# A banded attention and two feed-forward layers on one core: the order of a chunk's side jobs, with all float64 pieces ahead of both weights

## The chip, the cores and the metric

The kernel runs on 1 core of one Trainium2 chip. The metric is the device time of one execution in microseconds (us), as the median of several runs. The core's engines are named as in the profile: PE is the matrix engine (PEld its weight loads), DVE the vector engine, ACT the scalar engine, POOL the GpSimd engine, and SP the engine whose queue issues every DMA of this kernel.

## The reference, cut to what matters

Three layers follow each other on 2304 tokens of 512 values: an attention in which a query sees itself and the 127 positions before it, a layer of 8 experts whose gate is made doubly stochastic by 8 rounds of row and column scaling, and a dense layer with a leaky ReLU.

```python
for e in range(E):                       # E = 8 experts, F = 1024
    h = np.maximum(x @ w1[e], 0.0)
    out += P[:, e:e + 1] * (h @ w2[e])
...
h = x @ w_in                             # 512 x 2048
return np.maximum(0.01 * h, h) @ w_out   # 2048 x 512
```

The weights of the experts arrive as float32. The weights of the dense layer, `w_in` and `w_out`, arrive as float64, so the kernel turns them into float32 itself.

## The kernel before, in words

**The long stage.** After the attention, the kernel works through 20 chunks `ci`: 16 of them are halves of an expert (512 columns of `w1`, 512 rows of `w2`), the last 4 are quarters of the dense layer. The tokens are cut into five groups `p`; four hold two pairs of 128-token tiles and one, `p == 4`, holds one pair. For each chunk and group there is a first product (`a_steps`, L686 on) and a second one (`b_steps`, L817 on). Each product of 2 by 2 blocks is made with seven block products, each of them a "step" of six matmuls of 256 columns (twelve of 128 in the first product of group 4). A step's result is read out of PSUM by ACT and DVE, and the low halves of the float16 operands are made on POOL (L794).

**The order of units.** The main loop (L1015 to L1067) walks over units `(ci, p)`, from chunk 1 on in the order of `p` 0, 4, 1, 2, 3. A unit's first products are merged with the second products of the unit before it, so that the units 4, 1, 2, 3, 0 that follow each other have 21, 21, 28, 28 and 28 steps: 126 steps a chunk.

**Side jobs.** What is not on the way of the products is cut into small jobs in a list `side`. The list for the next chunk, `ci + 1`, is filled when unit `(ci, 4)` begins (L1041) and `tick` (L1055) hands out so many of them after each step that they are used up a fixed number of steps later:

```python
rest = {4: 57, 1: 36, 2: 8, 3: -19}.get(p) ...
tick(-(-len(side) // max(len(seq) - k + rest, 1)))
```

At the start of unit `(ci, 4)` that is 21 + 57 = 78 steps for the whole list. Where there are more jobs than steps, two jobs follow each of the first steps until the numbers are even. `pop` ties a job's instructions behind the last read-out that the steps have issued on each of ACT, DVE and POOL, so a job does not run earlier than its step; it can run later, since the program's final order on each engine is drawn up at compile time from when its inputs are expected. SP's loads and stores are not tied to steps: they stand in SP's queue in program order, and each waits there for its buffer.

**What the jobs do.** There are two kinds. A float64 piece (`to_single`, L628 to L680) is loaded as integers (512 KB, L644), goes through five jobs, `exponent` (DVE L650, ACT L653), `signed` (DVE L656), `high` (DVE L661, ACT L662), `low` (ACT L668, POOL L670) and `put` (POOL L674 and a store, L675), and ends in DRAM as float32. There are 32 pieces: three for each of the chunks 2 to 11, whose lists run during chunks 1 to 10, and two in the list that runs during chunk 11. The other kind are the chunk's two weights `a` (first product) and `b` (second product): a load of 1 MB (L565), then `scale()`, 16 or 17 jobs (four sums of squares on ACT, L569; a small reduction across partitions by way of PE and DVE, L421 to L441; four scalings on ACT, L572), then `early()`, 6 jobs (two splits into float16 halves, ACT L446 and POOL L447, and four block sums on POOL, L596). The remaining five splits of each weight (`at`) are made later, in the last steps of the chunk, as the weight tiles come free.

**The buffers.** Pieces and weights share two staging buffers, the tag `raw` of the pool `stg`. A piece gives its buffer back when its store has landed. A weight holds its buffer until its last split, at the end of the chunk. So of the five loads of a chunk's list, the first two wait for the two weights of the list before, and each other one waits for the store of a piece.

Of the kernel before, what the change touches and what calls it, by code (L numbers as in the profile page):

```python
# [31 lines left out]
def attn_moe_kernel(  # L32
# [591 lines left out]
    def weights(ci):  # L624
        for which in range(2):
            W[which][ci] = Weights(ci, which)
# [363 lines left out]
    def side_jobs(ci, n):  # L990

        todo = [to_single(cast.pop(0)) for _ in range(min(n, len(cast)))]
        weights(ci)
        a, b = W[0][ci], W[1][ci]
        jobs = [load for load, _ in todo[:2]]
        if not todo:
            return [a.load, b.load] + [None] * 10 + a.scale() + a.early() + b.scale() + b.early()
        jobs += [None] * 8 + todo[0][1] + [a.load]
        if len(todo) > 1:
            jobs += todo[1][1]  # L1000
        if len(todo) > 2:
            jobs += [todo[2][0]] + [None] * 4 + a.scale() + todo[2][1] + [b.load] + a.early()
        else:
            jobs += [b.load] + [None] * 8 + a.scale() + a.early()
        return jobs + [None] * 8 + b.scale() + b.early()

    def weigh(ci):
        pu[ci] = small.tile([P, NTILE], F32, tag="pu", name="pu")
# [12 lines left out]
    for n, u in enumerate(units + [None]):  # L1021
        a, b = [], b_steps(*prev)
        if u is not None:
            ci, p = u
            assert ci < NCE or p in split_pairs
            a = a_steps(ci, p)
            k0 = len(a) - 7
            if p == ends[ci] and ci + 1 < NC:
                a = [[f] + ([lambda j=k - k0: W[0][ci + 1].at(j)] if k >= k0 else []) for k, f in enumerate(a)]
            else:  # L1030
                a = [[f] for f in a]
        if prev[1] == ends[prev[0]] and prev[0] + 1 < NC:
            k0 = len(b) - 7
            b = [[f] + ([lambda j=k - k0: W[1][prev[0] + 1].at(j)] if k >= k0 else []) for k, f in enumerate(b)]
        else:
            b = [[f] for f in b]
        if u is not None and ci >= 1:
            if n and units[n - 1][0] != ci and ci != NCE:
                weigh(ci)
            if p == 4:  # L1040
                side += side_jobs(ci + 1, 3 if ci < NCE - 1 else 0) if ci + 1 < NC else []  # L1041
# [65 lines left out]
```

## Time and profile before

| | |
|---|---|
| median of 3 runs | 1924.01 us (1923.15 to 1927.62) |
| the profiled execution: its time | 1925.29 us |
| the profiled execution: its span | 1923.5 us |
| instructions in the span | 45099 |
| PE busy | 1852.1 us (96%) |
| ACT, DVE, POOL busy | 1363.4, 1314.2, 1325.4 us |
| granted PE clock over the span | 0.995 of full speed |

The span is the time from the first to the last instruction of the profiled execution; its own time is 1.8 us longer. A row of the timeline gives the start of an instruction, its duration, its engine, the line of the kernel, what it writes and reads, and in square brackets how long the engine had been idle before it and what ended the idle time. Matmuls are pipelined and their ends are modelled, so a short pause of PE shows less idle time than it costs; the period from one chunk to the next shows the whole.

### The profile page before, as it was taken

How to read it: one execution, taken by the hardware profiler on the slowest of the kernel's cores; microseconds unless marked ns; L12 is line 12 of the kernel's file. 1: busy time of each engine (PE TensorE's matmuls, PEld its weight loads, DVE VectorE, ACT ScalarE, POOL GpSimd, SP SyncE). 2: the span in 40 equal slices, each digit the busy share in tenths (PEclk: the TensorE clock that was granted, in tenths of full speed). 3: DMA queues.
4: the chain of work that ended last, by engine and by line, in shares of the span. 5: the costliest groups of instructions: out<-in, count | busy, mean ns of one | idle time of the engine just before them, and what ended most of it. 6: DMA issues, size and time to landing. Idle time of an engine off the chain costs nothing.

```text
span 1923.5 us, 45099 instructions
## 1 busy us (share of the span) xinstructions
PE 1852.1 (96%) x17725; PEld 1609.8 (84%) x17725; DVE 1314.2 (68%) x3606; ACT 1363.4 (71%) x3125; POOL 1325.4 (69%) x1142
## 2 busy tenths in 40 slices
PE   7899898999999999999999999999999998999998
PEld 5677787888888888988888888988889787888897
DVE  5456566766776767767676777666666786677776
ACT  7978667776767767676776767666666779776764
POOL 3843566867768686877868777685767786665753
PEclk8999999999999999999999999999999999999999
DMA  7522002021111202111111201100001010101001
GB/s 230 171 89 83 2 12 83 26 69 55 45 63 39 70 26 83 30 65 67 40 56 40 83 23 56 45 24 23 23 24 45 1 45 1 45 2 45 2 29 72
DMA packets 57861, 97.80 MB, mean 51 GB/s; under 512 B 3632, under 2 KB 22064, under 8 KB 57648
## 3 DMA queue, kind: packets, MB, share of 16 engines
q1 hardware_dynamic: 57648, 94.92, 15.1%
q8 instruction: 138, 2.26, 0.5%
q14 instruction: 75, 0.61, 0.1%
HBM read 81.81 MB, written 13.11 MB: 49 GB/s over the span
## 4 chain that ended last, share of the span: by engine, by line
PE 76%; ACT 9%; DMA 5%; DVE 5%; POOL 3%; issue 2%; SPq 0%; POOLq 0%; DVEq 0%; ACTq 0%
PE t L838 35%; PE s L721 21%; PE sq L721 15%; DMA raw<-in_moe_w_dram 4%; ACT junk L569 2%; ACT e L261 1%; PE o L305 1%; DVE s L750 1%; PE pt L288 1%; PE s L249 1%; ACT raw L572 1%; POOL h L794 1%; ACT w L446 1%; DMA raw<-in_moe_w_in_dram 1%; POOL w L447 1%
## 5 line engine op out<-in xcount | busy, mean ns | idle before, releaser
L838 PE MATMUL t<-w,h 128*128 128x256 f16 x7560 | 981.2, 273 | 20.7 <-DVE acc L851 9.2
L721 PEld LDWEIGHTS <-w 128*128 128x128 f16 x8400 | 758.7, 98 | 111.0 <-issue 29.2
L838 PEld LDWEIGHTS <-h 128*128 128x128 f16 x7560 | 730.2, 98 | 118.7 <-issue 30.5
L721 PE MATMUL s<-xp,w 128*128 128x256 f16 (+1 forms) x4872 | 611.7, 262 | 18.1 <-ACT q L745 11.4
L851 DVE SCALAR_TENSOR_TENSOR acc<-t,pu,acc 128x256 f32<-128x256 f32 x864 | 407.6, 478 | 213.3 <-PE t L838 161.0
L794 POOL TENSOR_TENSOR h<-s,h 128x1024 f16<-128x1024 f32 x180 | 388.2, 2156 | 126.2 <-ACT h L791 85.2
L721 PE MATMUL sq<-xp,w 128*128 128x256 f16 (+1 forms) x3528 | 451.9, 262 | 3.6 <-DVE s L750 2.6
L849 POOL TENSOR_TENSOR acc<-acc,part 128x256 f32<-128x256 f32 x324 | 235.2, 728 | 284.8 <-ACT part L848 256.7
L447 POOL TENSOR_TENSOR w<-raw,w 128x512 f16<-128x512 f32 x240 | 278.0, 1168 | 45.9 <-ACT w L446 45.6
L750 DVE SCALAR_TENSOR_TENSOR h<-sq,h 128x512 f16<-128x512 f32 (+1 forms) x352 | 192.8, 552 | 84.3 <-ACT h L775 48.4
L848 ACT ACTIVATE part<-t,pu 128x256 f32<-128x256 f32 x324 | 152.6, 471 | 110.0 <-PE t L838 102.1
L791 ACT ACTIVATE h<-s 128x1024 f16<-128x1024 f32 x180 | 189.7, 1054 | 43.7 <-DVE s L750 42.3
L737 DVE SCALAR_TENSOR_TENSOR sq<-sq,q 128x256 f32<-128x256 f32 x352 | 150.1, 427 | 61.4 <-PE sq L721 53.6
L733 ACT ACTIVATE q<-s 128x256 f32<-128x256 f32 x364 | 137.7, 380 | 70.9 <-PE s L721 59.1
L446 ACT ACTIVATE w<-raw 128x512 f16<-128x512 f32 x240 | 148.2, 628 | 8.3 <-PE t L838 6.0
L750 DVE SCALAR_TENSOR_TENSOR s<-sq,s 128x256 f32<-128x256 f32 x352 | 146.4, 416 | 2.0
L769 ACT ACTIVATE h<-sq 128x512 f16<-128x512 f32 x176 | 104.3, 593 | 55.7 <-PE t L838 30.4
L750 DVE SCALAR_TENSOR_TENSOR s<-sq,q 128x256 f32<-128x256 f32 x352 | 131.7, 415 | 13.5 <-ACT q L745 11.7
L737 DVE SCALAR_TENSOR_TENSOR sq<-s,q 128x256 f32<-128x256 f32 x176 | 75.3, 428 | 83.5 <-ACT q L733 78.4
L569 ACT ACTIVATE junk<-raw 128x512 bf16<-128x512 f32 x160 | 100.2, 627 | 44.1 <-DMA raw<-in_moe_w_dram 43.0
L775 ACT ACTIVATE h<-sq 128x256 f16<-128x256 f32 x176 | 66.7, 379 | 64.5 <-DVE sq L737 57.0
L572 ACT ACTIVATE raw<-raw,sr 128x512 f32<-128x512 f32 x160 | 102.4, 716 | 2.3 <-DVE sr L441 1.9
(137 smaller groups left out, 1712.3 us busy)
## 6 DMA issues: line engine op xcount, KB each, us to landing
raw<-in_moe_w_dram SPq DMA_DIRECT2D x32, 1024.0 KB, 5.1
k_t<-in_k_dram SPq DMA_DIRECT2D x16, 512.0 KB, 4.1
raw<-in_moe_w_in_dram SPq DMA_DIRECT2D x16, 512.0 KB, 3.6
raw<-in_moe_w_out_dram SPq DMA_DIRECT2D x16, 512.0 KB, 3.5
q_t<-in_q_dram SPq DMA_DIRECT2D x18, 256.0 KB, 4.1
v_t<-in_v_dram SPq DMA_DIRECT2D x18, 256.0 KB, 2.6
acc<-in_v_dram SPq DMA_DIRECT2D x18, 256.0 KB, 5.8
out_dram<-acc SPq DMA_DIRECT2D x18, 256.0 KB, 2.0
```

The costliest lines, as they stand in the source:

```text
L446: nc.scalar.activation(out=hi, in_=src, func=AF.Copy)
L447: nc.gpsimd.tensor_tensor(out=lo, in0=src, in1=hi, op=ALU.subtract)
L569: nc.scalar.activation(out=junk, in_=self.raw[:, k], func=AF.Square, accum_out=self.mx[:, k:k + 1])
L721: nc.tensor.matmul(d[b][:, f, :], t[:, wp, kk, ft * P:(ft + 1) * P], XP[p][:, o, kk, xp, :], start=(i == 0 and f == 0 and j in FIRST), sto ...
L737: nc.vector.scalar_tensor_tensor(out=block(k), in0=ps, scalar=CS, in1=q[:, k], op0=ALU.mult, op1=ALU.add)
L750: nc.vector.scalar_tensor_tensor(out=out, in0=in0, scalar=sc, in1=in1, op0=op0, op1=op)
L791: nc.scalar.activation(out=h[:, 3:7, 0, :], in_=d["s"], func=AF.Copy)
L794: nc.gpsimd.tensor_tensor(out=h[:, 3:7, 1, :], in0=d["s"], in1=h[:, 3:7, 0, :], op=ALU.subtract)
L838: nc.tensor.matmul(ps, h[:, o, hp, f, tt * P:(tt + 1) * P], w[:, wp, ft, :], start=(i == 0 and j in FIRST), stop=(i == 5), skip_group_chec ...
L848: nc.scalar.activation(out=part, in_=ps, func=AF.Copy, scale=s)
L849: nc.gpsimd.tensor_tensor(out=dst, in0=dst, in1=part, op=ALU.add)
L851: nc.vector.scalar_tensor_tensor(out=dst, in0=ps, scalar=s, in1=dst, op0=ALU.mult, op1=ALU.add)
```

## The change

Only the function `side_jobs` differs, which makes the list for one chunk; `n` is the number of float64 pieces (3, or the 2 that are left, or none). Without pieces the list is the same as before.

```diff
         jobs = [load for load, _ in todo[:2]]
         if not todo:
             return [a.load, b.load] + [None] * 10 + a.scale() + a.early() + b.scale() + b.early()
-        jobs += [None] * 8 + todo[0][1] + [a.load]
-        if len(todo) > 1:
-            jobs += todo[1][1]
-        if len(todo) > 2:
-            jobs += [todo[2][0]] + [None] * 4 + a.scale() + todo[2][1] + [b.load] + a.early()
-        else:
-            jobs += [b.load] + [None] * 8 + a.scale() + a.early()
-        return jobs + [None] * 8 + b.scale() + b.early()
+        loads = [load for load, _ in todo[2:]] + [a.load, b.load]
+        jobs += [None] * 8
+        for n, (_, cast_jobs) in enumerate(todo):
+            jobs += cast_jobs + [loads[n]] + ([None] * 8 if n == 1 else [])
+        jobs += loads[len(todo):]
+        return jobs + [None] * 3 + a.scale() + a.early() + b.scale() + b.early()
```

With three pieces the list was: loads 0 and 1, 8 empty jobs, piece 0, load a, piece 1, load 2, 4 empty jobs, scale a, piece 2, load b, early a, 8 empty jobs, scale b, early b (85 jobs). It becomes: loads 0 and 1, 8 empty jobs, piece 0, load 2, piece 1, load a, 8 empty jobs, piece 2, load b, 3 empty jobs, scale a, early a, scale b, early b (84 jobs). With two pieces the order of the loads stays and the empty jobs move (83 jobs before, 78 after).

## Rows read from the trace of the kernel before

**Rows 1.** The page: busy time by engine, and the chain that ended last by engine
```profile
PE 1852.1 (96%) x17725; PEld 1609.8 (84%) x17725; DVE 1314.2 (68%) x3606; ACT 1363.4 (71%) x3125; POOL 1325.4 (69%) x1142
...
PE 76%; ACT 9%; DMA 5%; DVE 5%; POOL 3%; issue 2%; SPq 0%; POOLq 0%; DVEq 0%; ACTq 0%
```

**Rows 2.** Stretches: length, busy us (instructions) PE, PEld, DVE, ACT, POOL, clock, DMA share, GB/s
```profile
278.00:363.20 85.20, 79.52 (x729) 69.23 (x728) 58.23 (x148) 64.71 (x141) 63.44 (x55) 1.00 0.17 54
363.20:1135.50 772.30, 759.00 (x7227) 671.51 (x7226) 547.87 (x1391) 541.27 (x1168) 589.86 (x495) 1.00 0.16 53
794.80:879.90 85.10, 83.98 (x804) 74.53 (x802) 60.56 (x155) 59.96 (x130) 65.53 (x55) 1.00 0.16 54
1135.50:1219.20 83.70, 83.70 (x805) 74.57 (x803) 59.51 (x153) 57.47 (x127) 62.65 (x53) 1.00 0.15 51
1301.40:1385.00 83.60, 83.60 (x805) 74.59 (x804) 54.24 (x146) 54.27 (x120) 57.38 (x50) 1.00 0.08 27
```

**Rows 3.** Waits over the whole span: waiter, waited for, us in total, times, longest
```profile
ACT junk L569 <- DMA raw<-in_moe_w_dram: 43.0, 22, 2.8
...
DVE raw L650 <- DMA raw<-in_moe_w_in_dram: 4.7, 5, 2.7
```

**Rows 4.** Timeline of ACT, 817 to 834 us
```profile
820.59 0.63 ACT L569 ACTIVATE junk<-raw 128x512 bf16<-128x512 f32 x1 [2.31 <-DMA raw<-in_moe_w_dram]
...
823.21 0.37 ACT L745 ACTIVATE q<-s 128x256 f32<-128x256 f32 x1
```

**Rows 5.** Timeline of PE, 817 to 834 us
```profile
823.63 1.70 PE L721 MATMUL s<-xp,w 128*128 128x256 f16 x12 [1.05 <-ACT q L745]
```

**Rows 6.** Timeline of ACT at two other waits of line 569
```profile
846.33 0.63 ACT L569 ACTIVATE junk<-raw 128x512 bf16<-128x512 f32 x1 [1.44 <-DMA raw<-in_moe_w_dram]
...
1163.82 0.63 ACT L569 ACTIVATE junk<-raw 128x512 bf16<-128x512 f32 x1 [1.54 <-DMA raw<-in_moe_w_dram]
```

**Rows 7.** Stretch from 840.7 us in chunk 7, columns as in rows 2
```profile
840.70:877.80 37.10, 37.10 (x339) 32.73 (x337) 23.65 (x66) 25.35 (x57) 34.60 (x30) 1.00 0.13 44
```

**Rows 8.** Timeline of SP's queue in the chunk from 794.8 us
```profile
813.38 0.33 SPq L675 DMA_DIRECT2D wout<-raw  x1
815.46 0.38 SPq L565 DMA_DIRECT2D raw<-in_moe_w_dram  x1
820.85 0.33 SPq L675 DMA_DIRECT2D wout<-raw  x1
822.98 0.33 SPq L644 DMA_DIRECT2D raw<-in_moe_w_out_dram  x1
839.21 0.33 SPq L675 DMA_DIRECT2D wout<-raw  x1
841.33 0.38 SPq L565 DMA_DIRECT2D raw<-in_moe_w_dram  x1
869.98 0.33 SPq L644 DMA_DIRECT2D raw<-in_moe_w_out_dram  x1
```

**Rows 9.** A piece's ACT and POOL groups: busy us, mean ns, idle before and its releasers
```profile
L662 ACT ACTIVATE raw<-raw,ones 128x512 f32<-128x512 int32 x32 | 22.9, 717 | 1.4 <-DVE raw L661 1.4
...
L670 POOL TENSOR_TENSOR raw<-raw 128x512 f32<-128x512 f32 x32 | 42.0, 1312 | 12.3 <-ACT raw L662 8.9 <-ACT raw L668 3.3
...
L674 POOL TENSOR_TENSOR raw<-raw 128x512 f32<-128x512 f32 x32 | 40.7, 1273 | 1.5
```

**Rows 10.** A piece's three DVE lines: duration ns min/median/max, first and last start
```profile
L650 DVE TENSOR_SCALAR raw<-raw x32: 411/654/2389, 273.2 to 1155.9; 128x512 int32<-128x512 int32 x32
...
L656 DVE SCALAR_TENSOR_TENSOR raw<-raw,sign x32: 741/1310/1800, 289.0 to 1157.8; 128x512 int32<-128x512 int32 x32
...
L661 DVE TENSOR_SCALAR raw<-raw x32: 408/417/2325, 286.5 to 1160.2; 128x512 int32<-128x512 int32 x32
```

**Rows 11.** Timeline of all engines, 826 to 831 us
```profile
826.84 2.14 POOL L794 TENSOR_TENSOR h<-s,h 128x1024 f16<-128x1024 f32 x1 [1.21 <-ACT h L791]
...
828.09 1.17 DVE L661 TENSOR_SCALAR raw<-raw 128x512 int32<-128x512 int32 x1
```

## The prediction

> **What bounds the kernel now.** I read the page first, then the waits, then the timeline around the largest wait on a DMA, then stretches cut at the chunk borders. The page says that PE is busy for 96% of the span and that the chain that ended last runs over PE for 76% of it [rows 1]. So only a pause of PE is worth anything, and the page does not say where PE pauses. The stretches do. They are cut where the matmuls of a unit `(ci, 4)` begin, which is where a chunk's list of side jobs begins: chunk 1 (most of it), chunks 2 to 10 together, chunk 7 alone, chunk 11 and chunk 13 [rows 2]. The reader should compare length and PE column. Chunk 13 has no pieces to convert, takes 83.6 us, and PE is never idle. Chunk 11 converts two pieces, takes 83.7 us, and PE is never idle either. Chunks 2 to 10 convert three each and take 772.3 us, 85.8 each; chunk 7, a quiet one among them, takes 85.1. So nine chunks at 83.7 would be 753.3 us, and 19.0 us is what three pieces in the present order cost. In chunk 1 PE is idle for 85.20 - 79.52 = 5.7 us [rows 2].
>
> The waits name the suspect: ACT stands 43.0 us in 22 waits for the DMA that brings expert weights, before line 569, the first job of `scale` [rows 3]. In chunk 7 the timeline shows how that reaches PE. ACT idles 2.31 us until 820.59, when weight a lands; the read-out L745, which stands behind that job in ACT's queue, ends at 823.58; PE, out of work, resumes at 823.63 after 1.05 us [rows 4, 5]. The chunk is 85.1 - 83.7 = 1.4 us over chunk 11, and its PE column lacks 1.1 us [rows 2], so this one pause is about all that chunk 7 loses. Not every such wait costs something: weight b's wait of 1.44 us at 846.33 lies in a stretch in which PE is busy all of the time [rows 6, 7], and the wait of 1.54 us in chunk 11 likewise [rows 2, 6]. What stands behind the waiting job decides.
>
> **The change, part by part.** *The list's length.* With three pieces 85 jobs over 78 steps become 84, so the first 6 steps and not 7 are given two jobs. With 126 steps in 83.6 us a step is 0.66 us [rows 2], so pieces 0 and 1 move by a step at most. Cost nothing; cover: PE's full queue.
>
> *Weight a.* Its first sum of squares moves from job 26 (step 19) to job 39 (step 33), and the load from job 15 to job 21: 17 jobs lie between load and use, not 10. But SP's queue does not follow the steps. Now the order is store 0, load a, store 1, load 2, store 2, load b; a load starts 2.1 us after the store whose buffer it takes [rows 8]. In the new order load 2 takes load a's place at 815.46 and load a takes load 2's place at 822.98. So weight a lands 7.5 us later than now, near 822.98 + 5.1 = 828.1, if the load takes what it takes now (815.46 to the use at 820.59) [rows 4, 8]. Step 33 begins 21.9 us after 794.8, at 816.7; the present load is used at 820.6 although step 19 begins at 807.4. The use is asked for 14 steps (9.3 us) later and the data come 7.5 us later, so the wait shrinks by 1.8 us, from 2.31 to about 0.5, or is laid elsewhere by the compiled order. It also moves from 26 us into the chunk to 33, into the unit of 28 steps, where first and second products alternate, as they do at weight b's wait, which cost nothing. So I take the whole pause of a quiet chunk, 1.4 us, as removed in each of ten chunks: 14.0 us. Its ends: nothing, if PE meets the same pause at the new place; and 19.0 + 5.7 = 24.7 us, if all that chunks 1 to 10 lose goes with it.
>
> *Piece 2.* It moves from step 35 to step 24, and its load from 822.98 to about 815.5, so it runs where weight a's sums ran. It brings three ACT instructions of about 0.72 us, two POOL ones of 1.31 and 1.27 us [rows 9], and on DVE 0.65 + 1.31 + 0.42 = 2.4 us by medians [rows 10]. Its own waits for DMA were small: 4.7 us in five waits, the longest 2.7 [rows 3]. None of these instructions is new; what can be new is that read-outs queue behind them in a unit where two first products come to each second one. The nearest rows are the waits that cost PE 0 and the one that cost 1.4. I take 0.2 us a chunk for this and what is left of weight a's wait, near the lower end because two of the three waits seen cost nothing: 2.0 us. Ends: 0 and 14 us.
>
> *Weight b.* Its load goes from step 40 to 29, and follows store 2 as before. `scale` and `early` of b stay at steps 55 and 72. With store 2 some 7.5 us earlier, load b starts near 834, and the wait at 846.33 goes. Gain 0, since PE did not feel it [rows 6, 7]. In chunk 1 it may have; that is inside the upper end.
>
> *`early` of a.* Its two splits and four block sums move from step 41 to 49, and by data 7.5 us, into the time in which POOL is 34.60 of 37.10 us busy [rows 7]. I take 0: 2.5 us of idle time and piece 2's 2.6 us, gone from just before, are cover. If that cover is gone, the splits of weight a that follow are late, and then the next chunk's first products: ends 0 and 7.5 - 2.5 = 5.0 us a chunk.
>
> *Chunk 11* (83 jobs become 78): the loads keep their order, piece 0 begins 5 steps later; nothing to gain, and PE's full column covers it. Left uncovered it costs one pause of 1.4 us.
>
> **Sum.** -14.0 + 2.0 = -12.0 us. The profiled execution took 1925.29 us (span 1923.5 and 1.8 around it), so it would take 1913.3; it lies 1.3 over the median of the runs shown, 1924.01, and against that the sum gives **1912.0 us**.
>
> **Rivals.** *The wait moves and costs the same.* The load of a starts later by the clock, not earlier, and 22 waits show that compiled order and data do not meet [rows 3, 8]. If PE pauses 1.4 us for weight a at its new place, nothing is won: about 1924. Against: the wait's size by the steps, and that two of three such waits were free. That the change does not do what it says (loads that wait on buffers are not issued earlier by being listed earlier) ends in this same case.
>
> *Piece 2 is held up by POOL.* A DVE line of a piece takes 0.42 us as a rule and up to 2.3 [rows 10]; at 828.09 one took 1.17 us, until 829.26, while POOL ran line 794 until 828.98 [rows 11]. If each of the ten moved pieces meets one more line 794, DVE loses 2.14 - 0.42 = 1.7 us a chunk, and if PE feels all of it, 17 of the 14 are given back: 1927. For it: the place is dense in read-outs by DVE. Against: piece 2 meets line 794 today already. The Trainium skill ("SBUF — State Buffer", section "SBUF: two separate sides") says that DVE and GpSimd share one port pair as an exclusive lock, so that the later of the two waits for the whole instruction of the other. By that rule, the trace agrees in the one case shown, and the sum would be this rival's 1927 and not 1912.
>
> *POOL is late with weight a* (the other side). From 840.70 to 877.80 POOL has only 2.50 us free [rows 7], and the next list's load 0, which waits for the last reading of weight a, starts at 869.98 [rows 8], as the next chunk's first unit is about to use it. If the shift of 7.5 us does not fit in, half of the upper end, 2.5 us a chunk, would reach PE: 25 - 12 = +13, 1937. It decides from 1.2 us a chunk on, where it eats the gain; from 1.8 us the kernel is measurably slower. Against: PE is full in all of that stretch today.
>
> **How the numbers follow.** Two results of this kernel can be told apart from about 0.3%, here 5.8 us. Chances: the forecast 0.62; the wait that moves 0.18; piece 2 held up 0.07; POOL late 0.13. The first is faster, the next two lie within 5.8 us of 1924, the last is slower: 0.62, 0.25 and 0.13. For the range: the lower end takes the upper gain of 24.7 less the 2.0, so about 1901; the upper end must take in both middle cases, 1924 and 1927, with the 1.4 us of chunk 11, so 1929. Outside are most of POOL's case and a little below.
>
> **What would show it.** Right: chunks 2 to 10 near 84 us each; line 569's waits well under 43.0 us, or moved to some 33 us into a chunk with PE full; in SP's queue store 0, load 2, store 1, load a. The forecast falls if chunk 7 stays at 85 us: then the row of PE's waits tells which rival, L745 or another ACT read-out (the moved wait), a DVE read-out near piece 2 with long L650, L656 or L661, or the splits of line 446 and 447 between 65 and 80 us into the chunk (POOL).

## The result, and the profile after

The changed kernel takes 1939.93 us (median of four runs, 1936.72 to 1942.01), the kernel before 1924.11 beside it (four runs, 1923.15 to 1927.62): a ratio of 1.0084, interval 1.0072 to 1.0097. It is slower by some 16 us, where 12 less were forecast. The profiled execution took 1942.01 us with a span of 1940.0. One execution of all that are reported here, in the run with weight a's sums four steps later, was slow, at 6689.14 us, and is left out there.

The page of the changed kernel: busy time by engine, and the chain that ended last by engine.

```profile
PE 1854.3 (96%) x17725; PEld 1609.2 (83%) x17725; DVE 1328.8 (68%) x3606; ACT 1358.8 (70%) x3125; POOL 1323.1 (68%) x1142
...
PE 67%; ACT 11%; DVE 6%; DMA 6%; POOL 6%; issue 4%; SPq 0%; POOLq 0%; ACTq 0%; DVEq 0%
```

Against [rows 1] PE's busy time is the same (2 us more) and PE's share of the chain has fallen from 76% to 67%, which went to the other engines, DMA and issue: PE waits more, it does not work more. DVE is the one engine that is busier by much, by 14.6 us. The same stretches as in [rows 2] say where (chunks 2 to 10, chunk 3 alone, chunk 7 alone, chunk 11; columns as there):

```profile
359.50:1147.40 787.90, 762.08 (x7229) 672.25 (x7228) 563.79 (x1392) 537.97 (x1168) 588.51 (x496) 1.00 0.16 52
449.10:541.30 92.20, 86.94 (x809) 75.68 (x807) 65.12 (x156) 59.76 (x131) 66.48 (x57) 0.98 0.15 50
802.10:887.70 85.60, 83.47 (x799) 73.98 (x797) 61.47 (x153) 59.07 (x129) 65.48 (x55) 1.00 0.16 54
1147.40:1233.10 85.70, 83.98 (x791) 74.12 (x789) 56.59 (x149) 57.12 (x126) 62.41 (x53) 0.98 0.15 50
```

Chunks 2 to 10 take 787.9 us where they took 772.3, 15.6 more; chunk 11 takes 2.0 more (85.7 against 83.7). Up to chunk 2 the kernel is 3.7 us ahead (359.5 against 363.2), after chunk 11 it loses another 2.6 (1940.0 - 1233.1 = 706.9 against 1923.5 - 1219.2 = 704.3): -3.7 + 15.6 + 2.0 + 2.6 = 16.5, the difference of the spans. In chunk 7 PE lacks 85.60 - 83.47 = 2.1 us; it lacked 1.1 [rows 2]. The 15.6 us do not fall evenly. Chunk 3 of the kernel before:

```profile
451.10:536.90 85.80, 84.75 (x811) 75.17 (x809) 61.51 (x158) 60.24 (x130) 65.43 (x55) 1.00 0.17 53
```

Chunk 3 takes 92.2 - 85.8 = 6.4 us more, chunk 2 takes 1.7 more (89.6 against 87.9), and chunks 4 to 10, the quiet ones, take 606.1 against 598.6: 7.5 more, or 1.1 each.

The waits over the span, first two rows of the kernel before that were not shown, then those of the changed kernel that answer to them and to [rows 3]:

```profile
PE s L721 <- ACT q L745: 11.4, 13, 1.3
...
PE t L838 <- DVE acc L851: 9.2, 17, 2.6
```

```profile
ACT junk L569 <- DMA raw<-in_moe_w_dram: 26.5, 16, 3.8
...
PE t L838 <- DVE acc L851: 21.7, 24, 2.6
...
PE s L721 <- ACT q L745: 4.6, 7, 2.1
```

What the change was meant to do, it did: the wait for weights fell from 43.0 to 26.5 us, and PE's wait for the read-out behind it from 11.4 to 4.6. But PE now waits 21.7 us, not 9.2, for the read-out of DVE (L851): 6.8 won and 12.5 lost in these two rows. Over chunks 2 to 10 alone the second row is, before and then after:

```profile
PE t L838 <- DVE acc L851: 1.1, 4, 0.4
```

```profile
PE t L838 <- DVE acc L851: 13.9, 11, 1.6
```

Each of chunks 3 to 10 has one such pause of 1.43 to 1.62 us behind the third piece's L661, 12.4 us together; in the kernel before none of them has one longer than 0.42. The groups of a piece's DVE lines (busy us, mean ns) name what stands ahead of that read-out, before and then after:

```profile
L656 DVE SCALAR_TENSOR_TENSOR raw<-raw,sign 128x512 int32<-128x512 int32 x32 | 42.4, 1324 | 9.3 <-ACT raw L653 9.2
...
L661 DVE TENSOR_SCALAR raw<-raw 128x512 int32<-128x512 int32 x32 | 21.6, 676 | 0.0
```

```profile
L661 DVE TENSOR_SCALAR raw<-raw 128x512 int32<-128x512 int32 x32 | 45.9, 1435 | 0.0
...
L656 DVE SCALAR_TENSOR_TENSOR raw<-raw,sign 128x512 int32<-128x512 int32 x32 | 30.9, 964 | 6.2 <-ACT raw L653 6.1
```

The 32 instructions of L661 are the same work and take 24.3 us more; L656 gets 11.5 back. By pieces, over the ten lists of three: the second pieces' L661 takes 18.5 us where it took 4.1, nearly always beside L794, and the third pieces' 13.8 where it took 8.0, in all but the first list beside L674. Chunk 7 shows both. First SP's queue, which answers to [rows 8], and ACT's use of weight a, which answers to [rows 4]:

```profile
820.77 0.33 SPq L675 DMA_DIRECT2D wout<-raw  x1
822.85 0.33 SPq L644 DMA_DIRECT2D raw<-in_moe_w_out_dram  x1
828.78 0.33 SPq L675 DMA_DIRECT2D wout<-raw  x1
830.91 0.38 SPq L565 DMA_DIRECT2D raw<-in_moe_w_dram  x1
```

```profile
836.16 0.63 ACT L569 ACTIVATE junk<-raw 128x512 bf16<-128x512 f32 x1 [0.91 <-DMA raw<-in_moe_w_dram]
```

The order is the predicted one, and ACT stands 0.91 us for weight a where it stood 2.31. Now DVE, POOL and PE some 20 to 28 us into the same chunk:

```profile
822.86 0.48 DVE L851 SCALAR_TENSOR_TENSOR acc<-t,pu,acc 128x256 f32<-128x256 f32 x1
823.25 1.96 DVE L661 TENSOR_SCALAR raw<-raw 128x512 int32<-128x512 int32 x1
...
826.43 1.19 DVE L650 TENSOR_SCALAR raw<-raw 128x512 int32<-128x512 int32 x1 [0.88 <-DMA raw<-in_moe_w_out_dram]
827.54 1.49 DVE L661 TENSOR_SCALAR raw<-raw 128x512 int32<-128x512 int32 x1
...
829.55 0.47 DVE L851 SCALAR_TENSOR_TENSOR acc<-t,pu,acc 128x256 f32<-128x256 f32 x1
```

```profile
822.66 2.27 POOL L794 TENSOR_TENSOR h<-s,h 128x1024 f16<-128x1024 f32 x1 [1.23 <-ACT h L791]
826.04 1.30 POOL L670 TENSOR_TENSOR raw<-raw 128x512 f32<-128x512 f32 x1 [1.12 <-ACT raw L662]
827.42 1.33 POOL L674 TENSOR_TENSOR raw<-raw 128x512 f32<-128x512 f32 x1
```

```profile
830.08 1.14 PE L838 MATMUL t<-w,h 128*128 128x256 f16 x9 [1.52 <-DVE acc L851]
```

The L661 at 823.25 is the second piece's, beside L794. The third piece (piece 2) now begins while POOL still has the addition and the multiplication of piece 1 before it. L650 waits 0.88 us for its load and then takes 1.19 us, until 827.62, beside L670, which ends at 827.34; L661 takes 1.49, until 829.03, beside L674, which ends at 828.75. Both can take 0.41 [rows 10]. L851 stands behind them and one other line (L750), ends at 830.02, and PE resumes at 830.08. Three suspects are left: the load that DVE waits for, POOL's instructions that hold DVE, or weight a's new place.

The worst chunk is the third, with 92.2 us; it also has what no quiet chunk has, a wait of 3.75 us for weight b. ACT, PE, and the stretch behind it (columns as in [rows 2]):

```profile
501.96 0.63 ACT L569 ACTIVATE junk<-raw 128x512 bf16<-128x512 f32 x1 [3.75 <-DMA raw<-in_moe_w_dram]
```

```profile
503.00 0.86 PE L721 MATMUL s<-xp,w 128*128 128x256 f16 x6 [2.10 <-ACT q L745]
504.18 1.44 PE L838 MATMUL t<-w,h 128*128 128x256 f16 x6 [0.32 <-DVE acc L851]
...
510.15 1.47 PE L838 MATMUL t<-w,h 128*128 128x256 f16 x12
```

```profile
503.00:507.00 4.00, 3.68 (x20) 2.60 (x20) 2.27 (x6) 4.00 (x9) 0.56 (x1) 0.58 0.00 0
```

### The profile page after: what moved, and what is told of

Read it like the earlier page. It is cut to its first block, busy times and chain, and to the rows that moved or that the text cites. A ratio compares the mean times of both kernels' runs of the same rounds, so it can differ in the third digit from the quotient of the medians.

```text
span 1940.0 us, 45086 instructions
## 1 busy us (share of the span) xinstructions
PE 1854.3 (96%) x17725; PEld 1609.2 (83%) x17725; DVE 1328.8 (68%) x3606; ACT 1358.8 (70%) x3125; POOL 1323.1 (68%) x1142
## 4 chain that ended last, share of the span: by engine, by line
PE 67%; ACT 11%; DVE 6%; DMA 6%; POOL 6%; issue 4%; SPq 0%; POOLq 0%; ACTq 0%; DVEq 0%
PE t L838 31%; PE s L721 18%; PE sq L721 14%; DMA raw<-in_moe_w_dram 3%; ACT w L446 2%; ACT junk L569 2%; ACT raw L572 2%; DVE s L750 1%; ACT e L261 1%; POOL h L794 1%; PE o L305 1%; DVE h L750 1%; PE pt L288 1%; POOL w L447 1%; PE s L249 1%
## 5 line engine op out<-in xcount | busy, mean ns | idle before, releaser
L838 PE MATMUL t<-w,h 128*128 128x256 f16 x7560 | 980.5, 273 | 37.1 <-DVE acc L851 21.7
L838 PEld LDWEIGHTS <-h 128*128 128x128 f16 x7560 | 729.8, 98 | 136.1 <-issue 48.8
L851 DVE SCALAR_TENSOR_TENSOR acc<-t,pu,acc 128x256 f32<-128x256 f32 x864 | 407.2, 478 | 223.6 <-PE t L838 165.4
L794 POOL TENSOR_TENSOR h<-s,h 128x1024 f16<-128x1024 f32 x180 | 384.8, 2138 | 135.4 <-ACT h L791 91.5
L848 ACT ACTIVATE part<-t,pu 128x256 f32<-128x256 f32 x324 | 152.6, 471 | 114.6 <-PE t L838 108.7
L750 DVE SCALAR_TENSOR_TENSOR h<-sq,h 128x512 f16<-128x512 f32 (+1 forms) x352 | 192.1, 550 | 58.7 <-ACT h L769 33.7
L737 DVE SCALAR_TENSOR_TENSOR sq<-sq,q 128x256 f32<-128x256 f32 x352 | 149.3, 426 | 77.7 <-PE sq L721 61.9
L733 ACT ACTIVATE q<-s 128x256 f32<-128x256 f32 x364 | 137.6, 380 | 79.9 <-PE s L721 59.3
L750 DVE SCALAR_TENSOR_TENSOR s<-sq,s 128x256 f32<-128x256 f32 x352 | 145.5, 413 | 2.1
L750 DVE SCALAR_TENSOR_TENSOR s<-sq,q 128x256 f32<-128x256 f32 x352 | 131.6, 415 | 21.0 <-ACT q L745 19.6
L737 DVE SCALAR_TENSOR_TENSOR sq<-s,q 128x256 f32<-128x256 f32 x176 | 75.2, 427 | 66.3 <-ACT q L733 58.5
L569 ACT ACTIVATE junk<-raw 128x512 bf16<-128x512 f32 x160 | 100.2, 627 | 27.6 <-DMA raw<-in_moe_w_dram 26.5
```

The lines of the kernel that those rows point to most:

```text
L737: nc.vector.scalar_tensor_tensor(out=block(k), in0=ps, scalar=CS, in1=q[:, k], op0=ALU.mult, op1=ALU.add)
L750: nc.vector.scalar_tensor_tensor(out=out, in0=in0, scalar=sc, in1=in1, op0=op0, op1=op)
L794: nc.gpsimd.tensor_tensor(out=h[:, 3:7, 1, :], in0=d["s"], in1=h[:, 3:7, 0, :], op=ALU.subtract)
L838: nc.tensor.matmul(ps, h[:, o, hp, f, tt * P:(tt + 1) * P], w[:, wp, ft, :], start=(i == 0 and j in FIRST), stop=(i == 5), skip_group_chec ...
L848: nc.scalar.activation(out=part, in_=ps, func=AF.Copy, scale=s)
L851: nc.vector.scalar_tensor_tensor(out=dst, in0=ps, scalar=s, in1=dst, op0=ALU.mult, op1=ALU.add)
```

## The experiments

Each run was measured beside the kernel before on the same chip; its median there was 1921.96, 1923.09, 1923.01, 1921.74 and 1922.74 us in the five groups below. In the expectations, pieces are counted first, second, third; the code calls them 0, 1, 2. A miss is a time outside the range expected for the cause under test.

### First group: the change taken apart

**The change's loads, the old jobs.** Loads in the new order, but weight a's sums ahead of the third piece, with the old empty jobs.

```diff
-            jobs += cast_jobs + [loads[n]] + ([None] * 8 if n == 1 else [])
+            jobs += (a.scale() if n == 2 else []) + cast_jobs + [loads[n]] + ([None] * 4 if n == 1 else [])
...
-        return jobs + [None] * 3 + a.scale() + a.early() + b.scale() + b.early()
+        return jobs + ([] if len(todo) > 2 else [None] * 4 + a.scale()) + a.early() + [None] * 8 + b.scale() + b.early()
```

> The loads stand in the order of the change (load 2 before load a), the jobs in the order of before (scale a ahead of piece 2, pauses as before). Theory D (piece 2, started right behind piece 1, holds up DVE: its load is waited for 0.9 us and L650 and L661 grow from 0.4 to 1.2 to 2.0 us beside POOL, so PE pauses 1.8 us some 26 us into a chunk): piece 2 is pushed behind scale a, the pause at 26 us is gone, about 1924 or less. Theory P (weight a is prepared late, because its load starts 7.5 us later, and POOL is full when its splits are due): the load of a is as late as after the change, so about 1935 to 1940. Theory W (the wait of line 569 only moved): ACT waits longer than in the change, 1930 to 1940.

1925.34 us, ratio 1.0017 (1.0007 to 1.0028). The loss is nearly gone, with the loads in the change's order. PE's wait for L851 is 7.7 us over the span and 0.5 in chunks 2 to 10. Yet POOL holds the third piece's L661 here too (1.85 us beside L794 in chunk 7; 16.3 us over the ten lists of three, against 13.8 in the change). So a DVE line that is held costs PE time only where a read-out that PE is about to need stands behind it.

**The change's jobs, the old loads.** Weight a's load stands ahead of load 2, all jobs as in the change.

```diff
-        loads = [load for load, _ in todo[2:]] + [a.load, b.load]
+        loads = [a.load] + [load for load, _ in todo[2:]] + [b.load]
```

> The jobs stand in the order of the change (piece 2 ahead of scale a), the loads in the order of before (load a before load 2). Theory D: piece 2 gets its data 7 us later, so it no longer runs right behind piece 1; the pause at 26 us goes, and with weight a long there line 569 waits little: 1908 to 1920. Theory P: scale and early of a keep the late place that the change gives them, so about 1935 to 1940. Theory W: line 569 waits for nothing at a, so 1910 to 1920.

1930.65 us, ratio 1.0038 (1.0026 to 1.0051): half of the loss comes back, more than the cause tested (theory D, 1908 to 1920) had given and less than theory P had, though the third piece's load is now issued later still. DVE, POOL and PE in chunk 7 of this run:

```profile
829.60 1.05 DVE L650 TENSOR_SCALAR raw<-raw 128x512 int32<-128x512 int32 x1 [2.14 <-DMA raw<-in_moe_w_out_dram]
830.57 0.41 DVE L661 TENSOR_SCALAR raw<-raw 128x512 int32<-128x512 int32 x1
```

```profile
822.62 1.27 POOL L674 TENSOR_TENSOR raw<-raw 128x512 f32<-128x512 f32 x1
...
828.24 2.13 POOL L794 TENSOR_TENSOR h<-s,h 128x1024 f16<-128x1024 f32 x1 [1.35 <-ACT h L791]
```

```profile
831.38 0.38 PE L721 MATMUL s<-xp,w 128*128 128x256 f16 x2 [0.56 <-DVE sq L737]
```

DVE stands 2.14 us for the load, more than twice the 0.88 of the change, and PE pauses 0.56 us, a third of the 1.52. By that time POOL's work on the second piece (ended 823.89) is over: L650 is held by L794 alone, and L661 takes 0.41. This speaks against the load wait. The half of the loss that stays is in other waits: in chunks 2 to 10 PE waits 1.1 us for L851, but 5.9 for L848, 3.4 for L737 and 3.1 for L733.

**A longer pause ahead of the third piece.** 14 empty jobs for 8, so the list grows from 84 to 90 jobs and 12 steps take two.

```diff
-            jobs += cast_jobs + [loads[n]] + ([None] * 8 if n == 1 else [])
+            jobs += cast_jobs + [loads[n]] + ([None] * 14 if n == 1 else [])
```

> The change with 14 empty jobs in place of 8 between piece 1 and piece 2, so that piece 2 and both weights are asked for some steps (up to 4 us) later. Theory D: DVE finds load 2 landed and POOL done with piece 1, and at least half of the 16 us come back: 1924 to 1932. Theory P: weight a is later still, 1940 to 1950. Theory W: about 1938, a little less wait at line 569.

1936.06 us, ratio 1.0076 (1.006 to 1.0093), a miss. The denser list pushes the first two pieces together: in chunk 7 the first piece's L661 took 2.18 us beside L794, the second piece's 1.12 beside L670 of the first, and PE then waited 0.81 us for L851, while the third piece's L650 and L661 took 0.43 and 0.42. In chunks 2 to 10 PE waits 11.5 us for L851. The same collision, one piece earlier.

**Two pieces a chunk in the old order.** The kernel before, with two pieces in the lists from the fifth on.

```diff
-                side += side_jobs(ci + 1, 3 if ci < NCE - 1 else 0) if ci + 1 < NC else []
+                side += side_jobs(ci + 1, 0 if ci >= NCE - 1 else 2 if ci > 4 else 3) if ci + 1 < NC else []
```

> The kernel before, but three pieces only in the lists of chunks 1 to 4 and two in those of chunks 5 to 14, in place of three in ten chunks, two in one and none in three. Not a test of the change, but of what the trace of before says a third piece costs (85.8 us a chunk with three, 83.7 with two, 83.1 with none): 4 x 85.8 + 10 x 83.7 in place of 10 x 85.8 + 83.7 + 249.4, so 11 us less than before, about 1913. If two pieces cost as much as three in the other chunks: 1924 or more.

1926.26 us, ratio 1.0026 (1.0016 to 1.0037), a miss. The eight chunks from the fifth to the twelfth, columns as in [rows 2]:

```profile
618.70:1301.10 682.40, 674.08 (x6419) 597.38 (x6417) 468.72 (x1210) 460.37 (x1009) 500.98 (x424) 0.99 0.13 45
```

682.4 / 8 = 85.3 us a chunk. So the 83.7 of chunk 11, from which the prediction took what three pieces cost, is not what a chunk with two pieces takes.

### Second group: what holds DVE

**No POOL work on the second piece.** The changed kernel; the line numbers behind L670 are two higher in its rows. The second pieces leave out the addition of their low words and the multiplication by their factor.

```diff
-            nc.gpsimd.tensor_tensor(out=man, in0=man, in1=rest, op=ALU.add)
+            if n % 3 != 1:
+                nc.gpsimd.tensor_tensor(out=man, in0=man, in1=rest, op=ALU.add)
...
-            nc.gpsimd.tensor_tensor(out=man, in0=man, in1=d["fac"].bitcast(F32), op=ALU.mult)
+            if n % 3 != 1:
+                nc.gpsimd.tensor_tensor(out=man, in0=man, in1=d["fac"].bitcast(F32), op=ALU.mult)
```

> The changed kernel, but the second piece of each chunk leaves out its two POOL instructions (the addition of L670 and the multiplication of L674), so those pieces are stored without their low words and their factor. No DVE instruction changes, and load 2, which follows the store of the first piece, starts when it did. Theory 'POOL holds DVE' (L650 and L661 of the third piece last as long as the POOL instruction of the second piece beside them): the third piece's L650 and L661 take 0.41 us each (they took 1.19 and 1.49 in chunk 7), the pause some 26 us into a chunk shrinks from 1.7 us to at most 0.5, chunk 7 takes 84.0 to 84.5 us instead of 85.6, and the kernel about 1924 to 1930. Theory 'DVE waits for load 2' (the 0.7 to 1.8 us of L650 behind the DMA): wait and pause stay, and the kernel stays at 1936 to 1940. Theory 'weight a is prepared late': nothing changes at 26 us, 1938 to 1942.

1919.89 us, ratio 0.9987 (0.9977 to 0.9998): the whole loss is gone, and some more than the 1924 to 1930 expected. Stretches (chunks 2 to 10, and chunk 5 alone), PE's wait for the same read-out in chunks 2 to 10 (lines L840 and L853 here), and DVE in chunk 5:

```profile
358.50:1125.60 767.10, 758.49 (x7221) 670.85 (x7219) 546.00 (x1386) 536.97 (x1166) 564.21 (x477) 1.00 0.16 54
619.20:703.70 84.50, 84.03 (x804) 74.51 (x802) 60.69 (x155) 59.61 (x130) 62.68 (x53) 1.00 0.16 54
```

```profile
PE t L840 <- DVE acc L853: 1.0, 4, 0.4
```

```profile
640.37 1.96 DVE L661 TENSOR_SCALAR raw<-raw 128x512 int32<-128x512 int32 x1
...
643.98 0.43 DVE L650 TENSOR_SCALAR raw<-raw 128x512 int32<-128x512 int32 x1 [1.31 <-DMA raw<-in_moe_w_in_dram]
644.33 0.42 DVE L661 TENSOR_SCALAR raw<-raw 128x512 int32<-128x512 int32 x1
```

DVE does the same work and still stands 1.31 us for load 2, longer than the 0.88 of the change; but the third piece's L650 and L661 take 0.43 and 0.42, and PE's column lacks 84.50 - 84.03 = 0.5 us where chunk 7 of the change lacks 2.1. It was POOL's instructions on the second piece that held DVE and not the load, and the wait of 13.9 us for L851 went with them. The second piece's L661 (640.37) is still held, 18.4 us over the ten lists, beside the instruction of L794 (L796 here); so the second pieces' 18.5 us of the change cost PE next to nothing. Chunks 2 to 10 differ by 787.9 - 767.1 = 20.8 us, of which 606.1 - 592.0 = 14.1 lie in chunks 4 to 10, 2.0 each. Not all of that need be DVE's: POOL has 24.3 us less to do (588.5 - 564.2), the second piece is also stored sooner, and L569's waits are 15.8 us, not 26.5.

**The third piece three steps later**, in a list of the old length.

```diff
-            jobs += cast_jobs + [loads[n]] + ([None] * 8 if n == 1 else [])
+            jobs += cast_jobs + [loads[n]] + ([None] * 11 if n == 1 else [])
...
-        return jobs + [None] * 3 + a.scale() + a.early() + b.scale() + b.early()
+        return jobs + [None] * (0 if len(todo) > 2 else 3) + a.scale() + a.early() + b.scale() + b.early()
```

> The changed kernel with 11 empty jobs in place of 8 ahead of the third piece and none in place of 3 ahead of weight a's sums: the list is as long as before, and only the third piece and the loads behind it move, by three steps or 2.0 us. Theory 'DVE waits for load 2': the waits of L650 (9.2 us over the span) fall to nearly nothing, the pause at 26 us falls by about 0.9 us a chunk, and the kernel comes to about 1930. Theory 'POOL holds DVE': what counts is which POOL instruction runs beside L650 and L661; the second piece's are over by then, so the two lines shorten to about 0.4 to 0.7 us unless they meet an L794 or L849, and the kernel comes to 1924 to 1928. If DVE waits for no DMA any more and the lines stay long and the pause stays, the load wait is refuted as the main part. Theory 'weight a is prepared late': its sums move by no step, so 1938 to 1942.

1949.81 us, ratio 1.0142 (1.0126 to 1.0158): a miss for both. L650's waits for loads did fall (9.2 to 5.3 us) and the third pieces' L661 went from 13.8 to 8.1 us over the ten lists (0.96 us in chunk 7), but L569's waits rose to 40.7 us: the compiled order let the sums of weight a stand for data once more. PE's wait for L851 in chunks 2 to 10 fell to 7.1 us, that for L848 rose from 3.4 to 8.9, so much of this loss lies elsewhere than the change's.

**Weight a's sums four steps later** in the kernel before.

```diff
-            jobs += [todo[2][0]] + [None] * 4 + a.scale() + todo[2][1] + [b.load] + a.early()
+            jobs += [todo[2][0]] + [None] * 8 + a.scale() + todo[2][1] + [b.load] + a.early()
...
-        return jobs + [None] * 8 + b.scale() + b.early()
+        return jobs + [None] * (4 if len(todo) > 2 else 8) + b.scale() + b.early()
```

> The kernel before with 8 empty jobs in place of 4 ahead of weight a's sums and 4 in place of 8 ahead of weight b's: loads and pieces keep the order of the kernel before, the list is as long, and weight a's sums, the third piece behind them and load b go four steps or 2.7 us later, more than the 2.31 us that L569 waited in chunk 7. This tries the prediction's largest term alone, that the wait for weight a costs a quiet chunk 1.4 us. If the term holds: L569's waits fall from 43.0 us to under 25, chunks 5 to 10 come to some 84 us and the kernel to 1908 to 1914. If what is lost is only laid elsewhere (the third piece, weight b or weight a's splits come later in the chunk and PE pauses there): the waits fall and the kernel stays at 1920 to 1926.

1952.18 us (median of three), ratio 1.016 (1.014 to 1.018): a large miss. SP's queue and ACT in chunk 7, which begins at 799.0 here:

```profile
825.73 0.38 SPq L565 DMA_DIRECT2D raw<-in_moe_w_dram  x1
...
860.06 0.38 SPq L565 DMA_DIRECT2D raw<-in_moe_w_dram  x1
```

```profile
830.65 0.63 ACT L569 ACTIVATE junk<-raw 128x512 bf16<-128x512 f32 x1 [1.62 <-DMA raw<-in_moe_w_dram]
```

Weight a's load starts 26.7 us into the chunk, where it started 815.46 - 794.8 = 20.7 [rows 8], and weight b's 61.1, where it started 46.5. Five loads a chunk pass through two buffers, so what ends later in one chunk lets the next chunk's pieces begin later: the load moved along with its use, and 1.62 us of the wait stayed. That the buffers are the reason is read from the queue's order and not tested.

### Third group: two ways to a faster kernel

**The first piece earlier**, by two and by four steps, in the kernel before (4 and 4 empty jobs; 0 and 8 in the second run).

```diff
-        jobs += [None] * 8 + todo[0][1] + [a.load]
+        jobs += [None] * 4 + todo[0][1] + [a.load] + [None] * 4
```

> The kernel before with 4 of the 8 empty jobs ahead of the first piece moved behind weight a's load. Only the first piece and load a come earlier, by two steps or 1.3 us; the second piece, load 2, weight a's sums and all behind them keep their steps, so nothing of the two buffers' turn is put later (in the run where weight a's sums, the third piece and load b came four steps later, the next chunk's pieces came 5 us later too and the wait stayed). This tries the prediction's largest term alone again, that the wait for weight a costs a quiet chunk 1.4 us. If the term holds: L569's wait in chunk 7 falls from 2.3 to about 1.0 us, the pause from 1.2 us to 0.5 or less, chunk 7 from 85.1 to about 84.4, and the kernel to 1914 to 1918. If PE's pause there has another cause: 1922 to 1926. If the first piece's DVE lines now meet the splits of weight b on POOL (L447, 1.16 us each, up to 10 us into the chunk), they last 0.5 to 1.2 us longer, PE pauses near 8 us into a chunk, and what is won is lost: 1922 to 1932.

> The same with all 8 empty jobs moved: the first piece and load a come four steps or 2.7 us earlier, more than weight a's wait of 2.3 us. If the prediction's term holds whole: no wait for weight a in chunks 5 to 10, chunk 7 at 83.9 to 84.2, and the kernel at 1909 to 1914. If POOL holds DVE up at the new place (L447 and the L794 that runs from 11.0 to 13.2 us into chunk 7), the first piece is converted no earlier, load a starts where it did, and PE pauses once more: 1924 to 1936.

1932.28 us, ratio 1.005 (1.0035 to 1.0065), and 1945.26, ratio 1.0117 (1.0102 to 1.0132). L569's waits fell to 29.1 and 37.4 us, and others grew: L650 stood 14.5 and 18.6 us for loads, where it stood 4.7 [rows 3]. Both times lie above the range of every theory, the first by 0.3 us. That the first piece's DVE lines met POOL, as the last theory of each has it, is not shown.

**The second piece's POOL work on DVE**, in the changed kernel.

```diff
-            nc.gpsimd.tensor_tensor(out=man, in0=man, in1=rest, op=ALU.add)
+            eng = nc.vector if n % 3 == 1 else nc.gpsimd
+            eng.tensor_tensor(out=man, in0=man, in1=rest, op=ALU.add)
```

(the multiplication likewise)

> The changed kernel with the addition and the multiplication of each chunk's second piece on DVE and not on POOL. Nothing is left out; DVE gets two more lines of some 0.75 us a chunk (L493's of 256 columns take 0.73 to 0.78; twice the columns may take more), POOL loses two of 1.3. If POOL's two instructions beside the third piece are what holds DVE (as the run without them says), their place is free of POOL, L650 and L661 of the third piece take 0.4 us, and the two new lines take back some of it: 1922 to 1932. If DVE is simply full some 26 us into the chunk, the pause stays or grows: 1938 to 1945.

1947.02 us, ratio 1.013 (1.0113 to 1.0147), a miss. In chunk 7 L650 and L661 of the third piece took 0.43 and 0.42 us, as they should with POOL out of the way, but the two new lines cost DVE 0.68 and 0.88, and L569's waits went from 26.5 to 36.3 us. The collision went and the time did not follow: in chunks 2 to 10 PE's wait for this read-out fell from 13.9 to 6.4 us, but it now waits 8.3 us for L848, 6.2 for L415 and 4.7 for L733 (by the old line numbers). So this run does not confirm that the collision is worth the whole loss.

### Fourth group: smaller loads

**Weight a's load in quarters**, in the kernel before.

```diff
-            nc.sync.dma_start(self.raw, chunks[self.ci][self.which].rearrange("(k p) f -> p k f", p=P))
+            for k in range(0, KT, 1 if self.which == 0 and 2 <= self.ci <= 12 else KT): ...
```

> The kernel before, list and steps untouched; only weight a's load (for the weights that chunks 1 to 11 prepare) is four loads of 256 KB, one for each of the four sums of squares, in place of one of 1024 KB. The first sum then needs only the first quarter, which lands some 2 us after its issue where the whole took 5.1 us, about 2.5 us sooner: more than weight a's wait of 2.3 us in chunk 7. This tries the prediction's largest term, that this wait costs a quiet chunk 1.4 us, with no piece moved by a step. If the term holds: L569's waits fall from 43.0 us to under 20, the pause 27.5 us into chunk 7 (1.2 us) goes, chunks 5 to 10 come to 83.9 to 84.3, and the kernel to 1908 to 1914. If PE pauses for another reason there, or the next thing is late at once (the third piece's load, DVE beside POOL): 1920 to 1926. If the three further issues on SP (0.38 us each) hold up the stores behind them: load 2 starts 1.1 us later and DVE waits for it, 1922 to 1930.

1932.29 us, ratio 1.0053 (1.0038 to 1.0068), a miss. ACT in chunk 7:

```profile
817.83 0.63 ACT L569 ACTIVATE junk<-raw 128x512 bf16<-128x512 f32 x1 [0.52 <-DMA raw<-in_moe_w_dram]
...
819.32 0.63 ACT L569 ACTIVATE junk<-raw 128x512 bf16<-128x512 f32 x1 [0.28 <-DMA raw<-in_moe_w_dram]
...
821.21 0.63 ACT L569 ACTIVATE junk<-raw 128x512 bf16<-128x512 f32 x1 [1.17 <-DMA raw<-in_moe_w_dram]
```

Chunk 7 begins at 793.1 here. The first quarter is used 24.7 us into the chunk, 1.1 us sooner than the whole was (25.8) [rows 2, 4]. The first quarter's load is issued 22.1 us into it, where the whole was at 20.7 [rows 8], and a quarter lands 3.6 us after its issue by median, not 2. The sums stand 0.52 + 0.28 + 1.17 = 1.97 us, against 2.31.

**Both weights' loads in quarters**, in the changed kernel.

> The changed kernel with both weights' loads in quarters in the same way (weights that chunks 1 to 11 prepare). The pieces' order is the change's. The wait for weight a (0.9 us in chunk 7, 26.5 us over the span with weight b's) should nearly go, and with it the pauses some 37 us and 51 us into the chunks. If what the change lost lies at the third piece, as the run without the second piece's POOL instructions says: the pause at 26 us stays at 1.5 to 1.8 us, and the kernel comes to 1928 to 1936. If the weights' waits were the greater part of the loss: 1915 to 1926.

1943.44 us, ratio 1.0107 (1.009 to 1.0124), above the 1928 to 1936 expected. DVE, POOL and PE in chunk 6:

```profile
738.72 0.61 DVE L650 TENSOR_SCALAR raw<-raw 128x512 int32<-128x512 int32 x1
739.26 1.50 DVE L661 TENSOR_SCALAR raw<-raw 128x512 int32<-128x512 int32 x1
```

```profile
737.76 1.29 POOL L670 TENSOR_TENSOR raw<-raw 128x512 f32<-128x512 f32 x1 [1.12 <-ACT raw L662]
739.13 1.34 POOL L674 TENSOR_TENSOR raw<-raw 128x512 f32<-128x512 f32 x1
```

```profile
743.12 0.82 PE L838 MATMUL t<-w,h 128*128 128x256 f16 x6 [1.65 <-DVE acc L851]
```

Here L650 waits for no load at all, L661 lasts until 0.29 us after L674, and PE pauses 1.65 us, as in the change: without a load wait the pause is still there. Four DVE lines, L656 among them, stand between this L661 and L851, so the pause is not shown to be L661's alone. Weights that come in parts do not help.

### Fifth group: the open term

Quarters with weight a's sums two steps later (6 empty jobs for 4, and 6 for 8 ahead of weight b's), and halves.

> The kernel before with weight a's load in quarters (chunks 1 to 11) and weight a's sums, the third piece and load b two steps (1.3 us) later: 6 empty jobs in place of 4 ahead of the sums and 6 in place of 8 ahead of weight b's. In the run with quarters alone the sums stood 0.5, 0.3 and 1.2 us for their quarters in chunk 7; two steps are 1.3 us. If the wait for weight a costs what the prediction says, and nothing new is late: no wait of L569 over 0.3 us near 27 us into chunks 5 to 10, chunk 7 at 83.9 to 84.4, and the kernel at 1910 to 1916. If the two buffers' turn is what gives way, as with four steps: the next chunk's pieces come later, the waits stay, 1928 to 1950.

> The kernel before with weight a's load (chunks 1 to 11) as two loads of 512 KB. Between the whole (1923) and the quarters (1932). If the loss with quarters came from three more issues ahead of the stores on SP and from quarters that land no sooner: this gives 1923 to 1929. If the compiled order puts the sums earlier by as much as the first half lands earlier, the waits of L569 near 27 us stay at 1.5 to 2.3 us in sum, and the kernel is within 1920 to 1932. If the first half's landing some 1.5 us sooner counts, the pause goes from 1.2 us to under 0.5 and the kernel to 1912 to 1918.

1931.10 us, ratio 1.0045 (1.0028 to 1.0062), and 1931.25, ratio 1.0049 (1.0034 to 1.0064). L569's waits are 36.0 and 34.4 us over the span. Six edits of the old list or of its loads tried to take this wait away; each changed the compiled order, and the wait came back in part at the new place. What it costs the kernel before by itself stays open: no run took it away and left the rest as it was. None of the kernels that compute the whole beats the kernel before.

## Why the prediction was wrong

**The step that failed** is "I take 0.2 us a chunk for this and what is left of weight a's wait ... 2.0 us", the price of piece 2 in its new place, "near the lower end because two of the three waits seen cost nothing". The waits seen were ACT's, and the new one is DVE's. The text placed piece 2 "where weight a's sums ran" without asking what POOL does there; the store of piece 1 at 820.85 [rows 8] says that POOL's last line of that piece ends just before. With the second piece's POOL work left out, nine chunks take 20.8 us less, 2.3 us a chunk where 0.2 was taken, and more than the upper end of 14. Part of those 20.8 are shorter waits for weights and less work for POOL; in chunks 4 to 10 it is 2.0 a chunk, and the pause of 1.52 us that the trace shows in chunk 7 is over seven times the 0.2.

**The rival that named the mechanism** got a chance of 0.07. "Piece 2 is held up by POOL" priced DVE's loss at 1.7 us a chunk, near the pause that came, and named L650, L656 or L661 as the lines that would be long. It took L794 for the partner, which piece 2 had met before, and so saw nothing new. The new partners are L670 and L674 of piece 1, which the change itself puts beside piece 2: before, weight a's sums lay between them. L794 did get a new partner as well, L661 of piece 1, but that cost PE next to nothing. The rival's 1927 is 13 us under what came; chunk 3 with its 6.4 us and chunk 11 were not in it.

**The 14.0 us for weight a's wait** did not come either. Its mechanism held: the queue's order, the load 830.91 - 802.1 = 28.8 us into chunk 7 where 20.7 + 7.5 = 28.2 was worked out, and a wait of 0.91 us for 0.5. Its size did not. In the run without the second piece's POOL work the nine chunks are 772.3 - 767.1 = 5.2 us better than before, 0.6 a chunk and not 1.4 (598.6 - 592.0 = 6.6 in chunks 4 to 10, 0.9 each), with less for POOL to do besides. Of the upper end of 24.7 us, 19.0 rested on chunk 11's 83.7 us; eight chunks of two pieces take 85.3 on average.

**The parts taken as nothing.** Chunk 11 lost 2.0 us, as its condition said ("Left uncovered it costs one pause of 1.4 us"): PE's full column was no cover, and PE pauses 1.54 us there for L848. Weight b's wait at 846 us went as predicted; that in chunk 3 went from 1.89 to 3.75 us and cost PE 2.10, which no step had. Why it grew is not shown. `early` of a was rightly put at nothing, at least in chunk 7: PE shows no wait from 867 to 882 us, where that rival had it. The rival in which POOL is late with weight a gave 1937, near the measured time, from a cause that did not act there; had it been the forecast, it would have been right by luck.

## What to carry to other kernels

When a change brings two pieces of side work together, look at what the engines do for the first while the second begins, not at each piece's cost alone: POOL's last instructions of one piece held DVE in the next, and a read-out that PE needed stood behind. DVE was held as long elsewhere and PE did not feel it, so the lines behind the held one decide. A wait that the trace shows is worth what the chunk without it takes, measured on several such chunks and not on one. Where loads turn through two buffers and the order is compiled anew for each edit, a use that is put later can go with a later load, and the wait stays.

## What the runs showed of the hardware

DVE beside POOL: in each case shown, an L650 or L661 that started during a POOL instruction ended some 0.28 us after it, whatever was left of that: L661 at 825.21 for L794's 824.93, L650 at 827.62 for L670's 827.34, L661 at 829.03 for L674's 828.75. So 0.41 us of work took up to 1.96. It is not two engines sharing a rate, but one that does its work when the other is done. Not every DVE line is held: L851, which reads `t` from PSUM, took 0.48 us at 822.86, inside the same L794 that held L661 until 825.21. The Trainium skill ("SBUF — State Buffer", section "SBUF: two separate sides") says that the two engines' shared port pair is an exclusive lock held for a whole instruction; the traces agree, and the run without POOL's instructions shows it by 0.43 and 0.42 us.

The granted clock: behind PE's pause of 2.10 us in chunk 3 it is 0.58 over the next 4 us, nearly the lower level (1.2 of 2.4 GHz), and six matmuls of L838 take 1.44 us where twelve take 1.47 some 6 us later. Behind the pause of 1.52 us in chunk 7 the clock of the chunk is 1.00. The length of the pause alone does not decide it: behind 1.62 us in chunk 6 the clock did not fall, behind 1.54 us in chunk 11 it was 0.57 from 1186 to 1190 us. Where it fell, a pause cost PE again after it had ended.
